# Moving the load and decoding of one piece of w_in behind unit 2's values, and giving unit 3's second value tile its own room, in a block-sparse attention and ELU feed-forward kernel on one core

## The chip, the cores and the metric

The kernel runs on one core of one Trainium2 chip. The time is the device time of one launch in microseconds (us): the median of several runs. A profile is one further execution, recorded by the hardware profiler.

## What is computed

Four sequences of 768 tokens with 8 heads of 64 attend under a block mask (blocks of 32: a window of one block to each side, the first and last block, and three sampled blocks per row of blocks). Its output, 3072 tokens of 512, goes through two dense layers with an ELU between.

```python
scores = scale * np.matmul(q, k.transpose(0, 1, 3, 2))
scores = np.where(mask, scores, -1000000000.0)
attn = np.exp(scores - np.max(scores, axis=-1, keepdims=True))
attn = attn / (np.sum(attn, axis=-1, keepdims=True) + 1e-09)
x = np.matmul(attn, v)          # then heads beside each other: 3072 x 512
h = x @ w_in                    # 512 x 2048
g = np.where(h > 0.0, h, np.exp(np.minimum(h, 0.0)) - 1.0)
return g @ w_out                # 2048 x 512
```

## The kernel before

The work is cut into 24 *units* of 128 query rows (two neighbouring blocks of 32 from two sequences). Unit 0 is a special one (the first and the last block); units 1, 2, 3 and so on are ordinary. Two units make one tile of 256 tokens for the dense layers. Matrix products in full precision are made of three 16-bit products, so every operand is split into a high and a low 16-bit part.

An ordinary unit `u` has these operations, called by short names: `q{u}` loads its queries; `vt{u}` and `vt{u}/2` load the two value tiles (one per block) on SP's queue, and `vg{u}`, `vg{u}/2` gather their sampled rows by an indirect DMA on GpSimd (POOL); `kg`, `kw` collect the keys on POOL; `s{u}.0`, `s{u}.1` are the score products on TensorE (PE); `mx` (row maximum, VectorE, DVE), `mb` and `ex` (bias and exponential, ScalarE, ACT), `pt` (transpose, PE), `ph`, `pl` (16-bit parts, DVE) follow; `av{u}.0`, `av{u}.1` are the products with the values; `nl`, `nx` scale them; `xt`, `xh`, `xl` turn and split the result. Then `h` and `o` are the two dense layers, with `a1` to `a5` for the ELU.

The weights come in 8 pieces of w_in (`wl0` to `wl7`) and 8 of w_out (`wl8` to `wl15`), 1 MB each. A piece is loaded by SP (`wl`), then decoded in place: `wu` (ACT) writes the common room `ZB`, `wb` (DVE) merges it, `wh` (ACT) makes the high part, `wlo` (DVE) the low part. The dense layers use the piece only after `wlo`.

The program is written for five engines (PE, ACT, DVE, POOL, SP). A planner (class `Plan`) puts all operations into one list, and each engine executes its own operations strictly in the order of that list; waits between engines are added from what is read and written. All loads of SP go through one hardware queue; SP has eight completion semaphores for them, and a load waits until the load eight before it has landed.

Value tiles live in three rooms of `VT`, taken in turn (`next_slot`, line 985); unit 1 alone uses two rooms in `GR` (slots 3 and 4, line 1227). A tile that takes a room of `VT` waits for the products of the unit that used that room. The first load of a room also brings the last block's rows (lines 1229 to 1232), so it is three DMAs of 130, 130 and 390 KB instead of one of 390 KB; the gather brings 96 rows of 4160 bytes more. `ST` is a staging room: it holds zeros at the very start and is taken next by the piece `wl14`.

PE's order around the change is: `s1.0`, `s1.1`, `pt1.0`, `pt1.1`, `s2.0`, `pt1.2`, `pt1.3`, `av1.0`, `s2.1`, `pt2.*`, `av2.*`, `s3.0`, `pt3.*`, `h0.0` (first dense product), `s3.1`, `av3.0`, `av3.1`, `s4.0` and so on; the dense layers of the first two tiles are then mixed into the attention of later units.

Of the kernel before, what the change touches and what calls it, by code (L numbers as in the profile page):

```python
# [11 lines left out]
F16 = mybir.dt.float16  # L12
# [339 lines left out]
}  # L352

LATENCY = 0.05
TAIL = {"DVE": 0.08, "ACT": 0.09}
LANDING = 1.8
DMA_FROM = 3.4
# [31 lines left out]
class Plan:  # L389
# [32 lines left out]
    def order(self):  # L422
# [14 lines left out]
        for op in reversed(self.ops):  # L437
# [4 lines left out]
            for d in {*op.deps, *op.after}:  # L442
                need = min(d.where.values()) + (d.dma + LANDING + d.slack if d.dma else 0.0) + LATENCY
                d.prio = min(d.prio, op.prio - need)
# [18 lines left out]
        def left_at(b):  # L463
# [3 lines left out]
            for o in (*b.writers, *b.readers):  # L467
                if o.end is None:
                    return None
                at = max(at, o.end + LATENCY)  # L470
            return at
# [30 lines left out]
        def enter(op):  # L502
# [5 lines left out]
            for e in op.where:  # L508
                op.at[e] = max([at] + [
                    d.end + (0 if d.eng == e and not d.dma else LATENCY) for d in op.deps])  # L510
                bisect.insort(waiting[e], (op.prio, op.n, op))
# [33 lines left out]
        while left:  # L545
            moved = False
            for eng, ops in waiting.items():
# [61 lines left out]
                if eng == "SP" and op.dma:  # L609
                    while ring and ring[0][0] <= t + dur:  # L610
                        ring.pop(0)
                    while ring and sum(n for _, n in ring) + op.pk > RING:
                        dur = max(dur, ring.pop(0)[0] - t)
                free[eng] = t + dur - (min(TAIL[eng], 0.3 * dur) if eng in TAIL else 0.0)
                op.end = t + dur
                if op.dma:
                    dma_free = max(dma_free, op.end) + op.dma
                    op.end = dma_free + LANDING + max(0.0, RANK["LATE"][TO(op)])
                    if eng == "SP":
                        ring.append((dma_free, op.pk))  # L620
                        landed += [dma_free + LANDING] * op.nd
                        heapq.heappush(events, dma_free - RANK["BACK"])
                for e in (free[eng], op.end + LATENCY, op.end):
                    heapq.heappush(events, e)
# [22 lines left out]
        return done  # L647

    def run(self):
        for _, op in self.order():  # L650
            for b in op.new:
                b.ap = b.make()
            op.fn(op.eng)
# [3 lines left out]
def kernel(  # L657
# [63 lines left out]
    def const(shape, dtype, name):  # L721
        return sb.tile(shape, dtype, tag=name, name=name)
# [40 lines left out]
    ST = const([P, 2, RW], I32, "ST")  # L763
    ZB = const([P, 2 * DM], I32, "ZB")
    nc.gpsimd.memset(ZB, 0)
    VV = [VT[:, 2 * i : 2 * i + 2] for i in range(3)]
    VV += [GR[:, y * 4 * RW : (y + 1) * 4 * RW].rearrange("p (c b x) -> p c b x", c=2, b=2) for y in range(2)]
    idx = const([P, NB], I32, "idx")
    cols = const([1, NPAIR, (NB - 2) * NR], I32, "cols")

# [214 lines left out]
    def next_slot():  # L985
        slot_n[0] += 1
        return (slot_n[0] - 1) % 3
# [90 lines left out]
    def unit(u):  # L1078
        g, i = u // NUP, firsts[u // NUP][u % NUP]
        two = (i, i + 1) if i else (0, NB - 1)  # L1080
        return g, i, [(x, n) for x in range(2) for n in two]
# [21 lines left out]
    spare = 1 if unit(0)[1] == 0 else 0  # L1103
# [58 lines left out]
    def attention(u, t, via, due):  # L1162
# [34 lines left out]
        elif sp:  # L1197
# [8 lines left out]
            for c in range(NKC):  # L1206
                vt = vts[c // 2]

                def load(e, c=c, vt=vt):
                    dst = VV[vt.slot][:, c % 2].rearrange("p b x -> p (b x)")  # L1210
                    r0 = BLK + c * P
                    if c < NKC - 1:
                        nc.sync.dma_start(dst, vd[g].ap[r0 : r0 + P, :])
                    else:
                        nc.sync.dma_start(dst[0:64], vd[g].ap[r0 : r0 + 64, :])
                        nc.sync.dma_start(dst[64:P], vd[g].ap[NB * BLK :, :])
                plan.add({"SP": 0.5}, tv, load, r=[vd[g]], w=[vt], dma=1.9, name=f"vt{u}",
                         nd=1 if c < NKC - 1 else 2)
            vin = vts
        else:  # L1220
            for y in range(2):
                i = i0 + y
                vt = Buf("VG" if u == spare else "VT", lambda: None)
                vin.append(vt)

                def load(e, i=i, vt=vt, y=y):
                    vt.slot = 3 + y if u == spare else next_slot()
                    two = VV[vt.slot].rearrange("p c b x -> p c (b x)")
                    if in_room.get(("v", vt.slot)) != g:
                        in_room["v", vt.slot] = g  # L1230
                        nc.sync.dma_start(two[96:P, 0, :], vd[g].ap[NB * BLK : (NB + 1) * BLK, :])
                        nc.sync.dma_start(two[0:BLK, 1, :], vd[g].ap[(NB + 1) * BLK :, :])
                    nc.sync.dma_start(two[BLK:P, 1, :], vd[g].ap[(i - 1) * BLK : (i + 2) * BLK, :])
                whole = first_in_room[u == spare] > 0
                first_in_room[u == spare] -= 1
                plan.add({"SP": 1.5 if whole else 0.6}, tv, load, r=[vd[g]], new=[vt], dma=2.7 if whole else 1.62, slack=RANK["SLACK"][2], name=f"vt{u}", nd=3 if whole else 1)

                def gather(e, i=i, vt=vt):
                    nc.gpsimd.indirect_dma_start(  # L1239
                        VV[vt.slot][0:96, 0].rearrange("p b x -> p (b x)"), None, vd[g].ap,  # L1240
                        bass.IndirectOffsetOnAxis(ap=idx[0:96, i : i + 1], axis=0))
                mark["vt", u] = plan.add({"POOL": 1.0}, tv, gather, r=[vd[g]], w=[vt], dma=1.65, slack=RANK["SLACK"][2], name=f"vg{u}")
# [456 lines left out]
```

## Time and profile before

| | us |
|---|---|
| median of 3 runs | 720.19 |
| lowest, highest run | 718.27, 724.62 |
| the profiled execution, its own time | 717.76 |
| its span, first to last instruction | 715.8 |
| PE busy | 675.0 |
| mean granted clock of PE | 0.984 of full |

The profiled execution's span is 2.0 us shorter than its own time, and that time is 2.4 us under the median of the three runs.

### The profile page before, as it was taken

Reading aid. Unit: us, or ns where it says so; the run is one execution under the profiler, and the core shown is the slowest. Engines: PE = TensorE matmul, PEld = TensorE weight load, DVE = VectorE, ACT = ScalarE, POOL = GpSimd, SP = SyncE. Lnnn points to the kernel's source line nnn. Section 1 sums busy time; section 2 is a strip of 40 time slices with the busy share of each in tenths; the row PEclk is TensorE's granted clock in tenths of the full one; section 3 lists DMA queues with packets and bytes.
Section 4 is the critical chain, followed back from the end, with each engine's and each line's share of the span. In section 5 each row is a group of like instructions: output and inputs, shape, how many; then the busy total and the mean of one; then the engine's idle time right before and its main releaser. Section 6 shows DMA issues by size and latency. Waiting matters only on the chain.

```text
span 715.8 us, 23435 instructions
## 1 busy us (share of the span) xinstructions
PE 675.0 (94%) x9586; PEld 452.0 (63%) x9586; DVE 457.1 (64%) x896; ACT 405.4 (57%) x815; POOL 212.4 (30%) x446
## 2 busy tenths in 40 slices
PE   8786779999999999999999999999999999999997
PEld 5564447666566567577567577587576476586673
DVE  4677798997667667667678567665367466354140
ACT  2765379895666556547377457365366365453250
POOL 2327255541022551100663432302044334000000
PEclk9997899999999999999999999999999999999999
DMA  8999999999899998877579998979669987871001
GB/s 194 241 365 224 252 288 246 245 208 252 201 207 208 195 173 158 172 188 186 114 107 187 185 187 154 165 152 196 120 120 209 183 133 126 149 114 31 16 2 30
DMA packets 200780, 123.18 MB, mean 172 GB/s; under 512 B 155936, under 2 KB 184736, under 8 KB 199904
## 3 DMA queue, kind: packets, MB, share of 16 engines
q1 hardware_dynamic: 195664, 103.98, 70.9%
q0 software_dynamic: 4928, 17.57, 10.4%
q8 instruction: 75, 1.23, 0.8%
q14 instruction: 33, 0.27, 0.1%
q10 hardware_dynamic: 80, 0.13, 0.0%
HBM read 76.98 MB, written 13.21 MB: 126 GB/s over the span
## 4 chain that ended last, share of the span: by engine, by line
PE 80%; DMA 6%; DVE 5%; issue 3%; ACT 3%; SPq 2%; POOL 0%; POOLq 0%; ACTq 0%; DVEq 0%
PE h L1559 32%; PE o L1585 28%; PE av L1459 6%; PE s L1585 3%; PE s L1346 3%; PE s L1355 3%; DMA wi<-in_moe_w_in_dram 2%; DMA VT<-vd,idx 1%; DMA vd<-ST 1%; SPq L945 1%; DMA wi<-in_k_dram 1%; PE av L1585 1%; PE s L1334 1%; DMA st<-in_k_dram 1%; DVE ST L1030 1%
## 5 line engine op out<-in xcount | busy, mean ns | idle before, releaser
L1559 PE MATMUL h<-xT,wi 128*128 128x256 f16 x2304 | 266.3, 273 | 5.9 <-DVE FE L1567 4.1
L1559 PEld LDWEIGHTS <-wi 128*128 128x128 f16 x2304 | 221.5, 98 | 47.2 <-issue 8.5
L1585 PE MATMUL o<-wo,GR 128*128 128x512 f16 x960 | 219.0, 379 | 0.1
L1585 PEld LDWEIGHTS <-GR 128*128 128x128 f16 x1152 | 109.6, 98 | 126.1 <-issue 5.0
L1286 POOL COPY kG<-kT 128x128 int32 x264 | 90.7, 380 | 154.3 <-PE s L1355 47.4
L1567 DVE SCALAR_TENSOR_TENSOR FE<-h,FE 128x512 f32<-128x512 f32 x96 | 65.4, 688 | 67.6 <-ACT FE L1572 67.3
L1388 DVE TENSOR_REDUCE m<-s 128x2 f32<-128x512 f32 (+1 forms) x104 | 65.4, 663 | 36.9 <-PE s L1355 20.4
L1156 DVE TENSOR_TENSOR p<-e,p 128x512 f16<-128x512 f32 x84 | 60.6, 721 | 42.8 <-ACT p L732 42.2
L1570 ACT ACTIVATE FE<-h 128x512 f32<-128x512 f32 x96 | 56.4, 594 | 55.6 <-PE h L1559 53.6
L1120 ACT ACTIVATE e<-s,m 128x256 f32<-128x256 f32 x176 | 73.4, 470 | 21.3 <-DVE p L1156 19.8
L1239 POOL DMA_INDIRECT VT<-vd,idx x42 | 43.2, 1029 | 140.1 <-PE av L1459 133.5
L1572 ACT ACTIVATE FE<-FE,gs 128x512 f32<-128x512 f32 x96 | 68.6, 721 | 2.0
L1577 DVE TENSOR_TENSOR GR<-FE,GR 128x512 f16<-128x512 f32 x86 | 62.2, 738 | 11.2 <-ACT GR L732 9.9
L732 ACT ACTIVATE GR<-FE 128x512 f16<-128x512 f32 x74 | 45.6, 628 | 23.4 <-DVE FE L1567 23.1
L732 ACT ACTIVATE p<-e 128x512 f16<-128x512 f32 x70 | 43.8, 626 | 14.8 <-DMA pT<-p 14.6
L1459 PEld LDWEIGHTS <-pT 128*32 128x32 f16 (+1 forms) x3384 | 40.6, 99 | 17.9 <-issue 16.1
L1265 POOL COPY kG<-kT 128x384 int32<-128x384 int32 x88 | 48.8, 582 | 0.1
L1416 ACT ACTIVATE m<-m 128x2 f32<-128x2 f32 x90 | 17.8, 200 | 51.8 <-DVE m L1388 42.0
L1459 PE MATMUL av<-VT,pT 128*32 128x66 f16 (+4 forms) x3240 | 45.1, 206 | 1.7 <-DMA VT<-vd,idx 1.7
L732 ACT ACTIVATE ro<-o 128x512 f32<-128x512 f32 x17 | 10.1, 597 | 51.3 <-PE o L1585 47.6
L1346 PE MATMUL s<-kG,qT 64*32 64x256 f32 x704 | 29.6, 409 | 9.7 <-ACT FE L1120 4.5
L1585 PE MATMUL s<-wo,GR 128*128 128x512 f16 x144 | 33.7, 379 | 0.1
(164 smaller groups left out, 596.6 us busy)
## 6 DMA issues: line engine op xcount, KB each, us to landing
VT<-vd SPq DMA_DIRECT2D x42, 390.0 KB
st<-in_q_dram SPq DMA_DIRECT2D x44, 128.0 KB
out_dram<-ro SPq DMA_DIRECT2D x43, 128.0 KB
wi<-in_moe_w_in_dram SPq DMA_DIRECT2D x4, 1023.0 KB
wi<-in_k_dram SPq DMA_DIRECT2D x8, 384.0 KB
wo<-in_v_dram SPq DMA_DIRECT2D x6, 512.0 KB
st<-in_v_dram SPq DMA_DIRECT2D x12, 256.0 KB
st<-in_k_dram SPq DMA_DIRECT2D x12, 256.0 KB
```

The lines of the kernel that those rows point to most:

```text
L732: nc.scalar.activation(dst, src, AF.Copy, scale=scale)
L1120: nc.scalar.activation(e32.ap[:, y, :], s.ap[:, y, :], AF.Exp, bias=m.ap[:, 6 + y : 7 + y], scale=SC, accum_out=m.ap[:, 2 + y : 3 + y] if ...
L1156: plan.add(LO, rank + 1, margin=mo, fn=lambda e: ENG[e].tensor_tensor(p.ap[:, 1, :], got(), p.ap[:, 0, :], op=ALU.subtract), r=[e32, p], w ...
L1286: nc.gpsimd.tensor_copy(dst[:, :, r * W : (r + 1) * W], src[:, :, bass.ds(at[r], W)])
L1388: nc.vector.tensor_reduce(m.ap[:, at + i.start : at + i.stop], ss[c].ap[:, i], axis=AX.X, op=ALU.max, negate=True)
L1459: nc.tensor.matmul(av[half].ap[rs, at : at + w], lhsT=pts[d].ap[:, pl * 4 + y * 2 + z, rs], rhs=room[:, z, x, h * VW + v0 : h * VW + v0 + ...
L1559: nc.tensor.matmul(h.ap[:, a, :], lhsT=w[:, wl, cs], rhs=x.ap[:, xl, cc, :], start=(n == 0), stop=(n == 3 * NCC - 1))
L1567: nc.vector.scalar_tensor_tensor(e32.ap, h.ap, -IH * GS, e32.ap, op0=ALU.mult, op1=ALU.min)
L1570: plan.add({"ACT": 0.6}, p0, lambda e: nc.scalar.activation(e32.ap, h.ap, AF.Exp, scale=IH), r=[h], new=[e32], name=f"a1{U}.{f2}")
L1572: plan.add({"ACT": 0.72}, p0, lambda e: nc.scalar.activation(e32.ap, e32.ap, AF.Relu, bias=gs_col, scale=-GS), r=[e32], w=[e32], name=f"a2 ...
L1577: plan.add(LO, p0, margin=mo, fn=lambda e: ENG[e].tensor_tensor(g.ap[:, 1], e32.ap, g.ap[:, 0], op=ALU.subtract), r=[e32, g], w=[g], name= ...
L1585: nc.tensor.matmul(o.ap, lhsT=g.ap[:, gl, f % 2, m * P : (m + 1) * P], rhs=wo[:, part, wl, (f % 2) * DM : (f % 2 + 1) * DM], start=(f == 0 ...
```

## The change

Nine operations are taken out of the planner's list and put back behind another one; in addition the second value tile of unit 3 gets the room `ST` (slot 5) in place of the next room of `VT`.

```diff
+MOVES = [
+    ("wl1", "vt2/2"), ("vt3/2", "vt3"), ("vg3/2", "vg3"), ("wu1", "xh1"), ("wb1", "xl1"),
+    ("wh1", "wb1"), ("wlo1", "mx3.0/2"), ("vt4/2", "vt4"), ("vg4/2", "vg4")]
+EXTRA = 3
...
     def run(self):
-        for _, op in self.order():
+        line = [op for _, op in self.order()]
+        named = {op.key: op for op in line}
+        for key, behind in MOVES:
+            line.remove(named[key])
+            line.insert(line.index(named[behind]) + 1, named[key])
+        for op in line:
...
+    VV.append(ST.bitcast(F16).rearrange("p c (b x) -> p c b x", b=2))
...
-                    vt.slot = 3 + y if u == spare else next_slot()
+                    vt.slot = 3 + y if u == spare else 5 if u == EXTRA and y else next_slot()
```

What this does to each engine's order (PE's doesn't change):

```
SP    before: wl1 q4 vt1 vt1/2 vt2 vt2/2 vt3 q5 q6 wl9 wl2 vt3/2 vt4 wl10 q7 wl3 wl12 vt4/2 vt5
SP    after:  q4 vt1 vt1/2 vt2 vt2/2 wl1 vt3 vt3/2 q5 q6 wl9 wl2 vt4 vt4/2 wl10 q7 wl3 wl12 vt5
POOL  before: vg3 kg3.0 kw3.0 kg3.1 kw3.1 kg4.0 vg3/2 vg4 kw4.0 kg4.1 kw4.1 kg5.0 kw5.0 vg4/2 vg5
POOL  after:  vg3 vg3/2 kg3.0 kw3.0 kg3.1 kw3.1 kg4.0 vg4 vg4/2 kw4.0 kg4.1 kw4.1 kg5.0 kw5.0 vg5
ACT   before: wh8 wu1 mb1.0 mb1.0/2 ex1.0 ex1.1 wh1 mb1.1 ... nl2.0 xh1 nl2.1 mb3.0 ex3.0
ACT   after:  wh8 mb1.0 mb1.0/2 ex1.0 ex1.1 mb1.1 ... nl2.0 xh1 wu1 wh1 nl2.1 mb3.0 ex3.0
DVE   before: mx1.0/2 wlo8 wb1 mx1.1 mx1.1/2 ph1.0 wlo1 ph1.1 ... nx2.0 xl1 mx3.0 mx3.0/2 nx2.1
DVE   after:  mx1.0/2 wlo8 mx1.1 mx1.1/2 ph1.0 ph1.1 ... nx2.0 xl1 wb1 mx3.0 mx3.0/2 wlo1 nx2.1
```

Unit 3's second tile is the first value tile in `ST`, so its load also brings the last block's rows, three DMAs in place of one. One room of `VT` fewer is taken by unit 3, so unit 4's second tile waits for unit 2's products in place of unit 3's; from unit 5 on each tile waits for the same products as before. `wl14` now waits for unit 3's products.

## Rows read from the trace of the kernel before

**Rows 1.** The page, part 1: busy time of each engine in the span.

```profile
PE 675.0 (94%) x9586; PEld 452.0 (63%) x9586; DVE 457.1 (64%) x896; ACT 405.4 (57%) x815; POOL 212.4 (30%) x446
```

**Rows 2.** Busy time by stretch; then PE's granted clock, DMA share, GB/s.

```profile
57.00:62.00 5.00, 0.63 (x9) 0.14 (x8) 2.96 (x4) 2.24 (x6) 3.22 (x10) 0.90 1.04 207
62.00:70.00 8.00, 7.12 (x73) 3.85 (x74) 6.66 (x11) 4.75 (x14) 5.51 (x11) 0.64 1.04 241
...
75.00:78.00 3.00, 0.00 (x0) 0.00 (x0) 0.87 (x2) 0.00 (x0) 0.00 (x0) 1.00 1.03 242
...
87.00:106.00 19.00, 14.22 (x318) 9.33 (x310) 18.02 (x32) 13.27 (x30) 8.99 (x23) 0.91 0.92 280
...
110.00:211.00 101.00, 100.95 (x1252) 68.03 (x1251) 80.01 (x136) 75.55 (x130) 33.66 (x61) 1.00 0.96 229
```

**Rows 3.** What PE waited for, 40 to 120 us: total, times, longest.

```profile
PE s L1346 <- ACT FE L1120: 4.5, 1, 4.5
...
PE s L1346 <- issue: 3.2, 1, 3.2
PE av L1459 <- DMA VT<-vd,idx: 1.7, 1, 1.7
```

**Rows 4.** The chain of work that ended last, 57 to 62.5 us.

```profile
46.37 13.31 DMA wi<-in_moe_w_in_dram
...
60.98 0.23 ACT m L1416 x2
...
62.08 0.63 PE s L1346
```

**Rows 5.** Timeline, unit 1: start, duration, engine, work, idle before it.

```profile
57.65 0.69 DVE L1388 TENSOR_REDUCE m<-s 128x2 f32<-128x512 f32 x1 [0.44 <-PE o L1182]
...
65.70 1.22 DVE L897 TENSOR_TENSOR wi<-wi 128x1024 f16<-128x1024 f32 x1
...
67.44 1.28 DVE L1150 TENSOR_TENSOR pT<-h,pT 128x512 f16<-128x512 f32 x2
...
70.61 0.95 PE L1459 MATMUL av<-GR,pT 128*32 128x130 f16 x71 [0.96 <-issue]
```

**Rows 6.** What SP's queue waited for, 30 to 140 us.

```profile
SPq L1233 <- PE av L1459: 8.7, 2, 5.5
...
SPq L1233 <- DMA wi<-in_moe_w_in_dram: 4.6, 1, 4.6
```

**Rows 7.** Timeline of SP: loads as they were issued.

```profile
59.69 0.30 SPq L1233 DMA_DIRECT2D GR<-vd  x1
...
79.79 1.77 SPq L879 DMA_DIRECT2D wo<-in_moe_w_out_dram  x1
81.60 0.47 SPq L875 DMA_DIRECT2D wo<-in_moe_w_in_dram  x1
87.66 1.94 SPq L1233 DMA_DIRECT2D VT<-vd  x2
```

**Rows 8.** DMA view: queue of instruction fetches, 75.3 to 75.4 us (packets, MB, share).

```profile
q8 instruction: 1, 0.02, 80.6%
```

**Rows 9.** DMA view, 81.2 to 92.2 us: rate in 40 equal slices.

```profile
GB/s 83 62 28 141 62 92 160 372 417 432 387 432 432 447 365 380 409 409 402 409 409 402 402 379 298 112 15 257 136 151 378 333 136 197 106 106 227 333 392 315
```

**Rows 10.** Timeline of ACT and DVE, units 2 and 3.

```profile
85.63 0.60 ACT L732 ACTIVATE xT<-h 128x512 f16<-128x512 f32 x1 [0.24 <-PE h L1527]
...
86.50 0.68 DVE L1540 TENSOR_TENSOR xT<-h,xT 128x512 f16<-128x512 f32 x1
87.12 1.29 DVE L1388 TENSOR_REDUCE m<-s 128x2 f32<-128x512 f32 x2
...
89.85 1.36 ACT L732 ACTIVATE ZB<-wo 128x1024 f16<-128x1024 bf16 x1
...
94.44 1.22 DVE L890 SCALAR_TENSOR_TENSOR wo<-wo,ZB 128x1024 int32<-128x1024 int32 x1
...
100.63 0.36 DVE L734 COPY low<-av 128x192 f32<-128x192 f32 x1 [0.57 <-PE av L1459]
```

## The prediction

> **What bounds the kernel now.** I read the busy times first: PE is busy for 675 of 716 us [rows 1], so the time is PE's work plus the holes in it. Then the stretches, to see where the holes lie. From 110 to 211 us PE is busy for 100.95 of 101 us, although DMA, DVE and ACT are loaded too [rows 2]. So a microsecond that PE gains before 110 us should reach the end, and a microsecond lost there as well. Before 110 us PE is nearly empty in two places: 57 to 62 us (0.63 us busy) and 75 to 78 us (0.00 us) [rows 2]. The list of PE's waits gives their sizes: 4.5 us on an exponential of ACT, 3.2 us with no releaser shown, and 1.7 us on a gather into a value tile [rows 3].
>
> The first hole has a chain [rows 4]: the load of w_in's piece 1 (wl1) takes 13.31 us and lands at 59.68; only then does ACT run wu1, which stands in its queue ahead of unit 1's bias, so that the bias comes at 60.98 and s1.1 goes on at 62.08. The maxima that the bias needs were complete at 57.65 + 0.69 = 58.34 [rows 5]. SP stands behind the same load: the last load of unit 1's second value tile waited 4.6 us for it and was issued at 59.69 [rows 6, 7], and the products with that tile begin at 70.61 after 0.96 us of waiting [rows 5]. From 87 to 106 us another engine is the bound: DVE is busy for 18.02 of 19 us [rows 2].
>
> **Unit 1, what is removed.** Two paths lead to av1.0, and the later one counts. By calculation: the bias can start at 58.4, 2.6 us earlier, and DVE loses wlo1 (1.22 us) ahead of the low parts that end at 67.44 + 1.28 = 68.72 [rows 5]; together 3.8 us. The other decoding step of DVE, wb1, lay beside the wait and gives nothing more. PE could have run av1.0 at 70.61 - 0.96 = 69.65, so this path comes to 65.8. Its bounds are 2.6 us (the exponential alone) and about 5 us, because 62 to 70 us ran at a granted clock of 0.64, partly the 1.2 GHz level after the hole [rows 2], and a shorter hole may spare some of that. By data: SP no longer waits 4.6 us, so the tile comes to 66.0. I take the later, **-4.6 us**.
>
> The second hole follows, inside s2.1 and not at its begin. In it the DMA view shows one packet of the queue of instruction fetches, moving at 75.3 us [rows 8]; I read the hole as PE waiting for its own instructions. If that fetch is asked for by PE's progress, it moves along with PE and the hole keeps its 3.2 us; bounds: the hole stays where it is (rival 1) or closes (rival 3). I take the move, since the DMA engines are as loaded before it as they will be (1.04 of their time at 62 to 70 us [rows 2]).
>
> The Trainium skill, "DMA: Bandwidth & Descriptors", section "Queues, rings and completion order", says that a DMA engine takes turns between the queues that have work for it, packet by packet. By that rule a fetch isn't held behind the whole backlog of SP's loads, which speaks against rival 1; the hole in the trace shows only that the fetch was late, not what it stood behind.
>
> **Units 2 and 3, what is added.** The decoding now stands behind xh1 and xl1. xh1 ends at 85.63 + 0.60 = 86.23, wu1 takes 1.36 us, to 87.59; xl1 ends at 86.50 + 0.68 = 87.18 [rows 10], so DVE waits 0.4 us for wu1. wb1 takes 1.22 us [rows 10] and wlo1 1.22 us [rows 5]. Queued behind them on DVE are mx3.0 and nx2.1, and from there DVE has hardly a gap until 106 us. On ACT, wh1 waits for wb1, and nl2.1, mb3.0 and ex3.0 stand behind it; this runs beside DVE's delay and is shorter than it. The cost is 0.4 + 1.22 + 1.22, **+2.85 us**. It would be 0 to 1.2 us if DVE had room there; in the row of mx3.0 it follows xl1 with no idle time [rows 10], so I keep the upper end. wl1 itself now has until 86.23 - 4.6 = 81.6 us; its bytes stand behind unit 2's tiles, which are complete in SP's queue before q5, so I charge nothing, with 0 to 2 us as bounds.
>
> **Unit 3's second tile.** Its load waited for unit 2's products (8.7 us in two waits of this line [rows 6]) and was issued at 87.66 [rows 7]; now it goes with vt3. PE's wait of 1.7 us goes [rows 3], but DVE paces that place: what it gains is the 0.57 us that it sat idle before nl3.0 [rows 10]. **-0.6 us**. On POOL one gather moves ahead of kg3.0; POOL is busy for less than half of 87 to 106 us [rows 2], so it costs nothing, and under 1 us if the keys were late. vt4/2 moves ahead of wl10 and its gather ahead of kw4.0: nothing waited for either. wl14 waits for unit 3's products, which end long before it is issued.
>
> **What stands behind the moved loads.** vt3/2 is now ahead of q5, q6, wl9 and wl2, and it is a whole load: 160 rows of 4160 bytes from SP and 96 from the gather, 1.07 MB, at the 241 GB/s of 62 to 70 us [rows 2] 4.4 us. wl9 and wl2 show as the stretch near 400 GB/s from 83.1 to 88 us [rows 9], so wl9 ends about 85.6. The lull before (seven slices at a quarter of that rate, [rows 9]) gives back up to 1.5 us, and the 1 MB that wl1 leaves open near 50 us, where the queue may run dry, costs up to 3: wl9 lands at 88.5 to 91.5. It is wanted: DVE comes to wb9 at 94.44 - 4.6 + 2.85 = 92.7, and wu9 ahead of it takes 1.36 us [rows 10], so it must be there by 91.3. I charge **+0.2 us** (0 to 2).
>
> **Sum.** -4.6 + 2.85 - 0.6 + 0.2 = -2.1 us at 106 to 110 us. Behind that PE has no holes until 211 us, so nothing is lost by the rows; 0 to 2 us could be, if a weight then comes too late for an earlier PE, and I take 0. The profiled execution, 717.76 us, becomes 715.6; the median, 2.4 us above it, becomes 720.19 - 2.1 = 718.1 us.
>
> **Rivals.**
> 1. *The second hole doesn't move; slower.* If PE still resumes at 78 us, because the fetch stands behind the backlog of loads, the first gain is gone and the decoding in units 2 and 3 is paid: +2.85 - 0.6 = +2.3, 722.5 us. It decides from a resumption later than 78.0 - 2.3 = 75.7. For it: the late fetch itself, and DMA engines full on both sides [rows 2, 8].
> 2. *wl9 becomes the late one.* Every us beyond 91.3 is lost on ACT and DVE; from 93.4 nothing is left, at 94.3 it is 721 us. For it: wl1 took 13.31 us in the same queue [rows 4]. Against it: wl9 is small against the lull that is filled. The Trainium skill, same page, section "Why a DMA increments its semaphore by 16 and not by 1", says that a load counts as landed only when each of its engines has finished, so one slow engine delays all of it; by that rule wl9 would land later than the mean rate says. No row here shows the engines singly.
> 3. *The second hole closes as well.* The loads in flight are smaller without wl1, so the fetch comes in time: -2.1 - 3.2, 714.8 us. Against it: the same bytes are moved by 80 us.
> 4. *The gain is lost behind 110 us*: 720.2 us. Against it: PE's full stretch [rows 2].
>
> **How the numbers follow.** Forecast 0.42 (its own range 716 to 720), rival 1 0.16, rival 2 0.12, rival 3 0.20, rival 4 0.10. The predicted time is the forecast's, 718.1. The range takes in rival 3's 714.8 less 1 us and rival 1's 722.5 plus half a microsecond; the runs of before alone spread over 6 us: 713.8 to 723. A change under 1% (7.2 us) is about what a measurement of this kernel can't tell from none. Faster by that much needs rival 3 and a larger first gain (half of rival 3's chance): 0.10. Slower by it needs rivals 1 and 2 together: 0.04. Same: 0.86.
>
> **What would show it.** In the changed kernel's profile: no wait of 4.5 us at s1.1 but one near 2 us (57.6 to 59.6); av1.0 near 66; PE's hole of 3.2 us inside s2.1 ending near 73.5; wu1 near 81.6 with no wait on its load; DVE full from 82 us on; no wait of av3.0 on its gather; wu9 without a wait on wl9, at 88 to 90 us; PE full from about 108 us. I am wrong if the hole still ends at 78, if ACT waits for wl9 or wl1 for more than 1 us, or if the time from 110 us to the end grows by what was gained before.

## The result

| | before | changed |
|---|---|---|
| median | 717.55 us (21 runs) | 719.09 us (21 runs) |
| ratio, 95% interval | | 1.0051 [1.0028, 1.0075] |
| profiled execution, its own time (span) | 717.76 (715.8) | 715.86 (713.9) |

The kernel became about half a per cent slower where 0.3 % faster was forecast. The profiled execution of the changed kernel was the fastest of its 21 runs, so its span says nothing on the change; I read it by places, not by its end. Two more profiles of the changed kernel and three more of the kernel before (below) show what is usual. Some executions of any kernel run over 1.5 % above its fastest; all ratios leave these out (the medians over all 21 runs differ by 0.2 %), and in k1 and c2 below the profiled execution was such a one, so only their ratios are used. A second series of the unaltered changed kernel (e1 below) gave 1.0012 [0.9967, 1.0057]: that there is no gain of 0.3 % rests on the first series, and the size of the loss is uncertain.

The page of the changed kernel, part 1 (compare [rows 1]):

```profile
PE 672.1 (94%) x9586; PEld 451.6 (63%) x9586; DVE 455.8 (64%) x896; ACT 405.7 (57%) x815; POOL 211.4 (30%) x446
```

Busy time by stretch, changed kernel (compare [rows 2]; the last three columns are PE's granted clock, DMA share, GB/s):

```profile
57.00:62.00 5.00, 3.57 (x52) 1.71 (x49) 4.35 (x7) 3.26 (x11) 3.68 (x10) 1.00 1.02 226
62.00:70.00 8.00, 5.94 (x157) 4.06 (x159) 6.58 (x12) 3.71 (x11) 6.63 (x18) 1.00 1.04 251
70.00:75.00 5.00, 0.99 (x20) 0.38 (x24) 1.64 (x3) 0.04 (x1) 0.83 (x2) 0.77 1.04 276
75.00:78.00 3.00, 2.07 (x49) 0.79 (x41) 1.99 (x8) 1.32 (x5) 0.82 (x3) 0.50 1.05 277
87.00:106.00 19.00, 14.94 (x318) 9.81 (x310) 18.30 (x32) 13.12 (x27) 9.58 (x24) 0.84 1.04 296
110.00:211.00 101.00, 100.86 (x1251) 67.78 (x1249) 80.08 (x136) 76.02 (x133) 32.31 (x58) 1.00 0.96 228
```

What PE waited for, 40 to 120 us (compare [rows 3]):

```profile
PE s L1356 <- issue: 4.0, 1, 4.0
PE s L1142 <- ACT e L1130: 3.3, 3, 1.7
PE av L1469 <- issue: 2.7, 2, 1.8
PE av L1469 <- DMA GR<-vd,idx: 1.9, 1, 1.9
...
PE s L1356 <- ACT FE L1130: 1.6, 2, 1.2
```

The first part went as forecast: the hole at 57 us is nearly gone (PE 3.57 of 5 us busy against 0.63), s1.1's wait is 1.2 us in place of 4.5, av3.0's wait on its gather is gone. But the wait with no releaser inside s2.1 is 4.0 us (before 3.2), and a second one of 1.8 us stands inside av2.0. The stretch with nearly no work has only moved, from 75 to 78 us to 70 to 75 us. The timeline of PE gives the places: s1.1 and av1.0 ahead, then av2.0 behind its hole, s3.0 and the first dense product h0.0 (compare [rows 5]):

```profile
59.11 1.07 PE L1356 MATMUL s<-kG,qT 64*32 64x256 f32 x24 [1.19 <-ACT FE L1130]
...
66.35 0.84 PE L1469 MATMUL av<-GR,pT 128*32 128x130 f16 x54 [1.86 <-DMA GR<-vd,idx]
...
83.37 0.24 PE L1469 MATMUL av<-VT,pT 128*32 128x66 f16 x3 [1.76 <-issue]
...
85.36 1.96 PE L1356 MATMUL s<-kG,qT 64*32 64x256 f32 x32
...
92.60 1.75 PE L1569 MATMUL h<-xT,wi 128*128 128x256 f16 x12
```

In the DMA view a packet of the queue of instruction fetches goes ahead of the end of each hole. It starts at 71.9 and at 80.3 us and ends 1.5 us before PE goes on; the two windows are 71.9 to 72.0 us and 80.3 to 80.4 us (compare [rows 8]):

```profile
q8 instruction: 1, 0.02, 75.9%
...
q8 instruction: 1, 0.02, 96.7%
```

The chain of waits shows the load of piece 1, now 21.67 us under way (13.31 before, [rows 4]), then a load of q5 that SP could issue only behind it; SP's timeline gives wl9 at 84.46 (79.79 before, [rows 7]):

```profile
59.92 21.67 DMA wi<-in_moe_w_in_dram
...
81.60 4.98 DMA st<-in_q_dram
```

```profile
72.50 11.15 SPq L1109 DMA_DIRECT2D st<-in_q_dram  x4
84.46 2.51 SPq L889 DMA_DIRECT2D wo<-in_moe_w_out_dram  x1
```

**Where the lead goes.** I sorted PE's matmuls and weight loads by start and counted. Whatever the kernel, the holes that follow such a fetch packet lie at the same counts, if there is one: 1704 (inside s2.1), 1957 (inside av2.0), 2211, 2463, 2718, which are 252 to 255 apart. The list of waits gives most of them no releaser, and those at 2718 one that differs from run to run, even for the same kernel. (PE also stands with no releaser at 1408, 1427 and 2546 in some profiles, 0.6 to 1.3 us, with no such packet ahead; these aren't counted.) I read the five counts as the borders between blocks of instructions that PE fetches one at a time. 1451 is the border before them. The means of four profiles of the kernel before and three of the changed one, in us at which PE passes each place:

```
                 s1.1   1451   1704   1957   2211   2463   2718  o0.1.0  48 matmuls on
before (4)       62.0   71.4   77.4   83.5   90.1  100.8  107.1  110.0   115.9
changed (3)      59.4   66.9   74.9   83.9   93.6  101.4  107.7  112.3   118.7
difference       -2.6   -4.5   -2.5   +0.4   +3.5   +0.6   +0.6   +2.3    +2.8
```

The lead of 4.5 us is gone by 1957. And the fetches that belong to the first two borders: PE's entry into the block ahead, the begin of the next fetch packet after it (in brackets how long after the entry), the passing of the border, and the hole at it (from the start of one instruction to that of the next, so 0.2 to 0.4 us more than in the list of waits). The runs from e1 on are explained in the next section:

```
                enters  fetch       passes 1704 hole   fetch       passes 1957 hole
before            70.7  75.4 (+4.6)   78.0  3.5        79.7 (+1.7)   84.7  0.0
b1_before         71.7  74.6 (+2.9)   77.2  0.0        80.2 (+2.9)   83.0  0.8
b2_before         72.0  73.5 (+1.5)   76.9  0.0        79.3 (+2.3)   82.9  0.0
b3_before         71.2  74.8 (+3.6)   77.5  2.6        80.5 (+2.9)   83.5  0.3
changed           66.5  71.9 (+5.4)   74.7  4.4        80.3 (+5.7)   83.4  2.0
e1_same           67.1  72.3 (+5.2)   75.1  4.1        81.2 (+6.0)   84.1  2.7
a2_after          67.1  72.4 (+5.2)   74.9  2.6        81.4 (+6.4)   84.2  2.6
e2_decode_only    66.1  71.2 (+5.1)   73.8  3.7        79.5 (+5.7)   82.5  2.0
e3_room_only      68.8  74.3 (+5.5)   77.0  3.5        82.4 (+5.4)   85.1  2.2
e4_wl9_first      66.5  71.6 (+5.1)   74.2  3.5        80.2 (+5.9)   82.7  2.7
n1_no_decode      68.1  73.1 (+5.0)   75.7  2.4        81.2 (+5.5)   84.0  2.2
n2_no_piece       67.2  72.9 (+5.7)   75.6  3.4        81.0 (+5.4)   84.0  1.8
c1_after_piece9.. 65.2  70.4 (+5.1)   72.9  3.9        78.6 (+5.7)   81.6  2.0
k2_same_no_piece  67.9  73.0 (+5.2)   75.7  2.9        78.5 (+2.8)   82.4  0.0
k3_after_room...  66.8  71.4 (+4.6)   73.9  3.3        78.9 (+5.0)   81.9  2.2
k4_unit3_values.. 67.4  72.7 (+5.2)   75.3  4.1        78.6 (+3.3)   83.6  0.0
k5_before_value.. 68.6  74.3 (+5.7)   77.2  4.5        81.9 (+4.8)   85.5  0.0
k6_after_queries. 66.3  71.1 (+4.8)   73.7  2.4        78.6 (+4.8)   81.2  1.4
```

Summed over the first four borders the holes are 3.6, 1.2, 0.1 and 3.1 us in the kernel before (mean 2.0) and 7.6, 7.0 and 5.6 us in the changed one (mean 6.7): 4.7 us more, as much as unit 1 gained. In these two blocks a fetch that starts 5 to 6 us after PE's entry costs a hole; one that starts 1.5 to 3.3 us after it costs at most 0.8 us. In between it depends on how long PE needs for the block (k5 took 8.3 us for its second one and shows no hole). Every hole of over 1 us at these two borders ends 1.2 to 1.7 us behind the end of its packet, in all profiles; this is what ties the holes to the fetches.

### The profile page after: what moved, and what is told of

It is laid out like the page before. It is cut to its first block, busy times and chain, and to the rows that moved or that the text cites. A ratio compares the mean times of both kernels' runs of the same rounds, so it can differ in the third digit from the quotient of the medians.

```text
span 713.9 us, 23435 instructions
## 1 busy us (share of the span) xinstructions
PE 672.1 (94%) x9586; PEld 451.6 (63%) x9586; DVE 455.8 (64%) x896; ACT 405.7 (57%) x815; POOL 211.4 (30%) x446
## 3 DMA queue, kind: packets, MB, share of 16 engines
q8 instruction: 75, 1.23, 0.7%
## 4 chain that ended last, share of the span: by engine, by line
PE 62%; DMA 14%; DVE 9%; issue 4%; ACT 4%; SPq 3%; POOLq 2%; POOL 1%; DVEq 0%; ACTq 0%
PE h L1569 25%; PE o L1595 22%; DMA pT<-p 4%; PE av L1469 4%; PE s L1595 3%; DMA wi<-in_moe_w_in_dram 3%; PE s L1356 2%; POOLq L1292 2%; DMA xT<-n 1%; DVE m L1398 1%; SPq L955 1%; DMA VT<-vd,idx 1%; DVE FE L1577 1%; PE s L1365 1%; DMA wi<-in_k_dram 1%
## 5 line engine op out<-in xcount | busy, mean ns | idle before, releaser
L1249 POOL DMA_INDIRECT VT<-vd,idx x41 | 40.7, 992 | 143.1 <-PE av L1469 136.9
```

## The experiments

In all diffs the list MOVES is that of the change unless shown; each ratio is to the kernel before, run on the same chip.

**Which part is it.** Theory A at this point: late fetches, the decoding on DVE and a late wl9 together eat the first gain. The expectations call the start of o0.1.0, a group of products just before PE fills up, the mark.

```diff
 e1_same: the changed kernel, unaltered
 e2_decode_only
-EXTRA = 3, moves of vt3/2 vg3/2 vt4/2 vg4/2
+EXTRA = -1, only the moves of wl1 wu1 wb1 wh1 wlo1
 e3_room_only
-moves of wl1 wu1 wb1 wh1 wlo1
+only the moves of vt3/2 vg3/2 vt4/2 vg4/2, EXTRA = 3
 e4_wl9_first
+    ("wl9", "vt3")
```

> The changed kernel again, unaltered, for a second profile and more times. The mark is the start of o0.1.0 (the group of 6 matmuls of 512 columns just before PE fills up, at 109.28 us before and at 110.38 us in the first profile of the changed kernel). Theory A (the first gain is real but is eaten by two holes in which PE waits for its instructions while the DMA engines are full, and the decoding and a late wl9 then cost more than is left): both holes again, 4 us inside s2.1 and 2 us inside av2.0, ACT waiting 1 to 2 us for wl9, mark 109.9 to 111. Rival B (the mark is where it was and the time grows behind 110 us): mark at 108 to 109.3. Ratio to before 1.002 to 1.008 by both.

> Only the five moves of piece 1 (load and decoding); unit 3's second tile and unit 4's stay where they were, in rooms of VT. Theory A: unit 1 gains its 4 us, the DMA engines run empty near 80 us as before, so there is no hole inside av2.0 (or one under 0.5 us) and no wait for wl9; av3.0 waits for its gather; the decoding still costs 2 to 3 us: mark 108.3 to 109.8, ratio 0.995 to 1.002. Rival C (the decoding in DVE's full stretch is the whole loss, the loads don't matter): mark 110 or later, ratio 1.003 to 1.008.

> Only the room of unit 3's second tile and the four moves of the value tiles; piece 1 is loaded and decoded where it was before. Theory A: the hole at s1.1 (4.5 us) is there, the DMA engines don't run empty near 80 us, a hole of 1 to 2 us inside av2.0 appears, wl9 comes at 91 to 93 and ACT waits for it up to 3 us; av3.0 doesn't wait: mark 109 to 111, ratio 1.000 to 1.006. Rival C: no loss without the decoding, mark 107.6 to 108.7 (1.7 us of av3.0's wait or DVE's 0.6 us gained), ratio 0.997 to 1.000.

> All nine moves, and wl9 taken ahead of unit 3's second tile in SP's queue. Theory A: ACT's wait for wl9 (1.46 us) goes; the DMA engines are as full, so the holes inside s2.1 and av2.0 stay: mark 109 to 110 (0.5 to 1.4 us earlier than the changed kernel), ratio 1.000 to 1.005. Rival 2 of the prediction alone (wl9's lateness is the whole loss): mark 108 to 109, ratio 0.996 to 1.000.

Measured: e1 1.0012 [0.9967, 1.0057], e2 1.0044 [1.0012, 1.0076], e3 1.0014 [0.9972, 1.0055], e4 1.0056 [1.0017, 1.0094]; marks 113.1, 111.0, 110.6 and 113.9, of which theory A had only e3's. In e4 wl9 goes out at 67.4 us and ACT no longer waits for it; this brings nothing, so its lateness is not the cause (rival 2 of the prediction falls). e2 came out as rival C said, and n1 below tests that rival. Each part alone loses its lead at the same two borders: e2 leads by 3.6 us at 1704 (73.8 against 77.4) and by 1.0 at 1957; e3, whose lead is 0.4 us at 1704, is 1.6 us behind at 1957, with piece 1 in its old place. So an early PE isn't needed for the late fetch: the earlier load of unit 3's tile alone does it too.

e3 missed at s1.1 as well: 4.5 us of waiting were expected there, since piece 1 hadn't moved, but its load came in at 57.3 us (59.3 to 59.8 in the kernel before) and PE waited 1.6 us:

```profile
57.41 1.37 ACT L743 ACTIVATE ZB<-wi 128x1024 f16<-128x1024 bf16 x1 [0.35 <-DMA wi<-in_moe_w_in_dram]
...
59.75 1.07 PE L1358 MATMUL s<-kG,qT 64*32 64x256 f32 x24 [1.62 <-ACT FE L1132]
```

e3 and k5 below, both without the move of piece 1, enter the block at 1451 2.6 and 2.8 us ahead of the kernel before. What brings the load in earlier there is open, and so is how much of unit 1's gain the move of piece 1 is worth.

**Was the first profile of before usual (one execution each).** Theory D: its hole at s1.1 was unlucky and is usually under 3 us.

```diff
 b1_before, b2_before, b3_before: the kernel before, unaltered
 a2_after: the changed kernel, unaltered
```

> The kernel before, unaltered, for its profile alone. Its first profile had a hole of 4.5 us at s1.1 (the load of piece 1 landed at 59.7 us) and the mark o0.1.0 at 109.3 us. Theory D (that hole was an unlucky execution, its usual size is 1.5 to 2.5 us, so the change had less to gain than I took): the hole under 3 us, piece 1 used by ACT at 57 to 58.5 us, av1.0 at 68 to 69.5 us. Rival (the hole is as large in every execution and the change loses elsewhere): 4 to 5 us again, av1.0 at 70 to 71 us.

> As b1_before: a further execution of the kernel before. Theory D: the hole at s1.1 under 3 us and the mark within 1.5 us of the other profiles of this kernel. Rival: 4 to 5 us.

> As b1_before: a further execution of the kernel before. Theory D: the hole at s1.1 under 3 us. Rival: 4 to 5 us.

> The changed kernel, unaltered, a third profile. Theory D with theory A: s1.1 with 1.6 us of waiting as in both profiles so far, a hole of about 4 us inside s2.1 and of about 2.5 us inside av2.0, the mark o0.1.0 at 110 to 113.5 us, later than in the profiles of the kernel before by 1 to 3 us.

What PE waited for in b1, 40 to 120 us:

```profile
PE av L1459 <- DMA VT<-vd,idx: 4.1, 1, 4.1
PE s L1346 <- ACT FE L1120: 3.1, 1, 3.1
...
PE av L1459 <- DMA GR<-vd: 2.0, 1, 2.0
...
PE av L1459 <- issue: 0.6, 1, 0.6
```

The wait at s1.1 is 3.1 to 3.5 us there and s1.1 resumes at 61.7 to 62.2 us: usual, so theory D falls. The hole inside s2.1 is not: 3.5, 0, 0 and 2.6 us. And av3.0 waits 3.0 to 4.1 us for its gather, not 1.7. The sum was made against one execution, and at two of its terms that one was off by 1 to 2 us. a2 has its mark at 113.4 us, within what was expected, and two holes of 2.6 us, the first smaller than the 4 us expected.

**What the decoding costs, and what the load costs.**

```diff
 n1_no_decode (n1 and n2 leave out work; the dense layer reads piece 0 where it read piece 1)
-wu1, wb1, wh1, wlo1
 n2_no_piece
-wl1, wu1, wb1, wh1, wlo1
```

> The changed kernel without the decoding of w_in's piece 1 (wu1, wb1, wh1, wlo1 are left out, the load stays; the dense layer uses piece 0 in place of piece 1). Theory A, that from 85 to 107 us DVE sets the pace in the changed kernel and the decoding in it eats the first gain: DVE loses 2.45 us of work and the 0.6 us that it stood before wb1, wb9 comes 2 to 3 us earlier (93.6 to 95 in place of 96.6), and o0.1.0 stands at 109 to 110.5 in place of 110.4 to 113.4 (mean 112.3); ratio to the kernel before 0.997 to 1.000. Rival, that the loads behind unit 2's values are what comes too late (wl9 lands at 92.5): wu9 and wb9 stay where they are, o0.1.0 at 111.5 or later, ratio 1.003 or more.

> The changed kernel with neither load nor decoding of piece 1 (the dense layer uses piece 0 in its place): 1 MB less in SP's queue between 60 and 82 us. Theory A, with late instruction fetches caused by the backlog of loads: PE's hole inside s2.1 falls from 2.3 to 4.0 us to 1.5 us or less and the one inside av2.0 (1.8 to 2.5 us) goes; wl9 is issued 3 us or more earlier; o0.1.0 at 105 to 107.5, the end 5 us or more below the changed kernel's (ratio 0.992 to 0.995). Rival, that the fetch is late whatever SP loads: the two holes keep 2 us or more each and only the decoding's 3 us are gained, o0.1.0 at 109 to 110.

Measured: n1 1.0051 [1.0011, 1.0092], o0.1.0 at 110.8; n2 1.0006 [0.9967, 1.0044], o0.1.0 at 109.6. With the decoding taken out the kernel is no faster within the noise of half a per cent, where theory A wanted 0.997 to 1.000; the mark comes at the early end of the changed kernel's 110.4 to 113.4, and wb9 stays where it was (96.7 against 96.6 us). So theory A as I had it falls. DVE's timeline in n1 shows why, in the idle time in brackets:

```profile
84.64 0.16 DVE L1505 TENSOR_SCALAR r<-av 128x4 f32<-128x4 f32 x1 [2.08 <-ACT low L743]
...
87.98 1.29 DVE L1400 TENSOR_REDUCE m<-s 128x2 f32<-128x512 f32 x2 [1.34 <-PE s L1358]
...
90.93 0.69 DVE L745 CAST pT<-s 128x512 f16<-128x512 f32 x1 [0.66 <-PE s L1144]
...
95.50 1.29 DVE L1400 TENSOR_REDUCE m<-s 128x2 f32<-128x512 f32 x2 [0.76 <-PE s L1358]
```

DVE now stands 4.8 us in 82 to 96 us in these four waits for a PE that is late from its holes; the 2.45 us of decoding fit into that. n2 tells the load: without the 1 MB the ratio falls by 0.45 %, about 3 us, which is at the edge of the noise of the two. But the two first holes stay (3.4 and 1.8 us; 1.5 or less and none were expected), and the mark is at 109.6, not at 105 to 107.5: this is what the rival had, that the fetch is late whatever SP loads. I put it down to the value tile of unit 3, 1.07 MB, which has taken the place; k2 below, where that tile comes later, bears this out for the second hole alone.

In the changed kernel's profile PE comes out of those holes at the lower clock. Busy time by stretch, first the changed kernel, then n1, then b1 (column PEclk as above):

```profile
80.00:84.00 4.00, 2.24 (x75) 1.89 (x75) 1.89 (x3) 0.33 (x1) 0.00 (x0) 0.50 1.05 210
84.00:88.00 4.00, 4.00 (x108) 2.24 (x106) 3.13 (x7) 2.01 (x3) 0.46 (x2) 0.50 1.24 167
88.00:92.00 4.00, 2.27 (x18) 1.80 (x11) 3.90 (x9) 3.04 (x8) 2.74 (x6) 0.50 0.96 348
```

```profile
84.00:88.00 4.00, 4.00 (x79) 2.24 (x82) 1.73 (x6) 0.93 (x2) 0.00 (x0) 0.50 1.19 182
88.00:92.00 4.00, 2.94 (x51) 2.70 (x47) 3.24 (x8) 2.19 (x7) 2.46 (x7) 0.50 1.02 331
```

```profile
80.00:84.00 4.00, 3.23 (x112) 2.18 (x114) 3.90 (x12) 1.55 (x6) 1.67 (x5) 1.00 0.93 122
84.00:88.00 4.00, 2.87 (x105) 1.97 (x91) 3.71 (x10) 2.46 (x8) 1.36 (x6) 1.00 0.95 370
88.00:92.00 4.00, 3.83 (x56) 2.61 (x55) 3.97 (x7) 1.39 (x2) 3.44 (x8) 1.00 1.08 308
```

From 80 to 92 us the changed kernel is granted 1.2 GHz (0.50), b1 2.4 GHz. b1 is the best of its four: the others were granted 0.50 to 0.73 from 80 to 84 us and 0.74 to 0.89 from 84 to 88, and 1.00 from 88 to 92. The changed kernel's second profile (e1) is at 0.50 throughout as well, its third (a2) between 0.50 and 1.00. The 32 products of s3.0 take 1.96 us in the one and, in b1's timeline, 1.09 us:

```profile
84.17 1.09 PE L1346 MATMUL s<-kG,qT 64*32 64x256 f32 x32
```

So s3.1 starts at 94.3 us (90.2 in b1), and from its maximum on DVE has hardly a gap up to o0.1.0 in the changed kernel; in b1 it stands once for 3.0 us, behind av3.0's wait for its gather.

**Taking DVE's work out of 87 to 107 us instead.**

```diff
 c1_after_piece9_late: MOVES of the change, and
 c2_before_piece9_late: these alone, EXTRA = -1
+    ("wu9", "ph4.1"), ("wb9", "pl4.1"), ("wu10", "ex4.3"), ("wb10", "wu10"),
+    ("wh9", "ex4.3"), ("wlo9", "wh9"), ("wu3", "a21.0"), ("wb3", "a31.0"),
+    ("wh3", "a10.1"), ("wlo3", "a51.0")
```

> The changed kernel with the decoding of w_out's piece 9 moved behind 107 us (pieces 10 and 3 one turn later), so that DVE has 2.44 us less to do between 87 and 107 us. Theory A: o0.1.0 comes 2 to 2.5 us earlier than in the changed kernel (about 110 in place of 112.3), and some of it is given back from 110 to 126 us, where DVE had only 1.6 us idle at one place: end 0 to 2.4 us below the changed kernel's. Rival, that DVE isn't what sets 85 to 107 us there: o0.1.0 at 111.5 or later.

> The kernel before with the same move of piece 9's decoding. Theory A: in the kernel before the same stretch waits for unit 3's second value tile (av3.0 1.7 to 4.1 us on its gather, to 99 to 102 us), not for DVE alone, so o0.1.0 moves by 0 to 1 us (109.3 to 110.5 before), and the end is the same or up to 2 us later. Rival, that DVE sets this stretch in both kernels alike: o0.1.0 2 us or more earlier, at 107 to 108.5.

Measured: c1 1.0143 [1.0085, 1.0200], o0.1.0 at 113.1; c2 1.0106 [1.0052, 1.0161]. It came out as the rival said and worse: 2.44 us less of DVE does not bring the mark forward, since the fetch for 2718 came 6.1 us after PE's entry, with a hole of 5.0 us; behind 110 us more was lost, which I put down to the moved decoding without having shown it. DVE alone does not set this stretch. c2 lost more than the 2 us expected at most.

**Is it the fetch.** Theory F: a fetch is served early where SP's loads have just run dry and about 5 us late where other loads fill that lull.

```diff
 k1_room_behind_wl9: the kernel before, EXTRA = 3 and
+    ("vt3/2", "wl9"), ("vg3/2", "vt3/2")
 k2_same_no_piece: k1 without wl1, wu1, wb1, wh1, wlo1 (leaves out work; piece 0 in place of piece 1)
 k3_after_room_behind_wl9: k1 and the moves of wl1, wu1, wb1, wh1, wlo1
 k4_unit3_values_behind_wl9: the moves of wl1, wu1, wb1, wh1, wlo1 and
+    ("vt3", "wl9"), ("vt3/2", "vt3"), ("vg3", "vt3/2"), ("vg3/2", "vg3")
 k5_before_values_behind_wl9: the four moves of k4 alone, EXTRA = 3
```

> The kernel before with unit 3's second tile in its own room, its load put behind wl9 and its gather behind that, nothing else moved (piece 1 in its old place). Theory F (a block of 256 PE instructions is fetched while the one ahead of it runs, and the fetch is served 0.6 to 2.4 us after PE comes into that block when SP's loads have just run dry, as at 79 to 81 us in the kernel before, and 4.4 to 5.4 us after it when other loads fill that lull, as in the changed kernel): the fetch near 80 us stays at +3 us or less, PE has no hole over 1 us inside av2.0, mx3.1 starts at 91 to 93.5 as before, and without av3.0's wait for its gather (1.7 to 4.1 us before) o0.1.0 stands 1.5 to 3 us earlier than before's mean of 110.0; ratio 0.995 to 0.999. Rival, that any earlier load of this tile costs what it gains: fetch at +4 us or more or wl2 and wl9 late, o0.1.0 at 110 or later, ratio 1.000 to 1.004.

> The kernel k1_room_behind_wl9 without piece 1's load and decoding (the dense layer uses piece 0 in its place), so 1 MB less in the queue from 46 to 80 us, and PE early at s1.1 as in the changed kernel. Theory F: the loads run dry some 4 us earlier, so the fetches of the blocks that PE meets inside s2.1 and inside av2.0 come at +3.5 us or less and the two holes are together 3 us or less (4.1 to 6.3 us in the changed kernel's runs); o0.1.0 at 107 or earlier, ratio 0.990 to 0.995. Rival, that the fetch takes about 5 us behind PE whatever is loaded: both fetches at +4.4 us or more, holes of 4 us or more together, o0.1.0 at 108.5 or later.

> The changed kernel with unit 3's second tile loaded behind wl9 and not ahead of q5 (unit 4's tile in its old place): the decoding behind unit 2's values as in the change. Theory F: PE comes to the blocks 3 to 4 us earlier than in the kernel before, but the loads run dry no earlier, so the fetch near 80 us is again served at 79 to 81 us, +4 us or more after PE's entry, and the hole inside av2.0 stays at 1.5 us or more; wl9 is issued near 79 us, o0.1.0 at 110 to 112, ratio 1.000 to 1.004. Rival, that the early load of unit 3's tile alone spoils the change: no hole over 1 us inside av2.0, o0.1.0 at 107 to 108, ratio 0.994 to 0.998.

> The changed kernel with both value tiles of unit 3 (their loads and gathers, 2.1 MB) put behind wl9, so that the loads run dry before PE comes to the block of instructions inside av2.0; piece 1 and its decoding as in the change, unit 4's tile in its old place. Theory F: the fetch that PE met inside av2.0 comes at +3 us or less after PE's entry (4.4 to 5.4 us in the changed kernel), no hole over 1 us inside av2.0, the granted clock from 84 to 92 us is 0.9 or more in place of 0.50, wl9 is issued by 77 us; o0.1.0 at 106.5 to 109 (112.3 in the mean of the changed kernel's profiles, 110.0 before), ratio 0.993 to 0.998. Rival, that the fetch takes about 5 us whatever is queued: a hole of 1.5 us or more inside av2.0, the clock at 0.5 to 0.7 behind it, o0.1.0 at 110 or later, ratio 1.000 or more. Rival, that unit 3's values now come too late: av3.0 waits 2 us or more on DMA, o0.1.0 at 110 or later.

> The kernel before with the same move of unit 3's value tiles and with the room of its own, piece 1 in its old place. Theory F: PE comes to its blocks as late as before (s1.1 at 62, s2.1 at 77 to 78), the fetch near 80 us at +2 us or less, the clock at 0.85 or more from 84 to 92 us, and the gather wait of av3.0 (1.7 to 4.1 us before) under 1.5 us; o0.1.0 at 108 to 110 (110.0 before), ratio 0.996 to 1.000, that is 2 us or more behind k4_unit3_values_behind_wl9, which has unit 1's wait removed as well. Rival, that moving piece 1 brings nothing even with a free queue: this kernel as fast as that one within 1 us.

Measured: k1 0.9994 [0.9959, 1.0029], between theory F and its rival; k2 0.9973 [0.9940, 1.0006], o0.1.0 at 108.5; k3 1.0026 [0.9984, 1.0068], 110.6; k4 1.0033 [0.9998, 1.0068], 113.4; k5 1.0031 [0.9997, 1.0066], 111.1.

For the border at 1957 theory F held: in k3 wl9 went out at 77.75 us and the fetch still started only at 78.9, 5.0 us after the entry, with 2.2 us of hole; in k2, with 1 MB less queued, and in k4, with unit 3's tiles out of the way, it started 2.8 and 3.3 us after it and the hole was gone. The fetch for 1704 stayed 5.2 us late in both. What did not follow either is the time. PE's waits and the stretches of k2 and of k4:

```profile
PE s L1359 <- issue: 2.5, 1, 2.5
...
PE h L1572 <- issue: 1.9, 1, 1.9
```

```profile
80.00:84.00 4.00, 4.00 (x130) 3.09 (x136) 3.27 (x8) 1.37 (x4) 1.83 (x3) 0.69 1.03 278
84.00:88.00 4.00, 2.89 (x85) 1.99 (x66) 3.81 (x10) 2.62 (x8) 1.69 (x7) 1.00 1.05 251
```

```profile
PE s L1364 <- issue: 4.6, 3, 3.8
PE s L1150 <- ACT e L1138: 4.0, 3, 2.4
PE s L1364 <- DVE x L1516: 3.5, 1, 3.5
```

```profile
80.00:84.00 4.00, 2.98 (x77) 2.05 (x76) 2.48 (x4) 0.05 (x2) 2.33 (x4) 0.50 1.02 273
84.00:88.00 4.00, 3.76 (x108) 2.31 (x108) 2.80 (x6) 2.16 (x3) 0.46 (x1) 0.65 1.05 211
```

With the hole at 1957 gone, k2 has its clock back by 84 us but stands 1.9 us at the next border, 2211 (in h0.0, fetch 5.5 us after the entry). k4 is at the lower clock from the hole at 1704 up to about 86 us, waits for exponentials that stand behind the decoding on ACT, and meets a fetch 5.0 us late and a hole of 3.9 us at 2718; the list of waits puts that hole down to DVE's x (in other runs to ACT's p, m or low), but in the changed kernel's profile and in k2, k3, k4 and k6 alike it ends 1.5 to 1.7 us behind the end of the fetch packet. k5 misses its own expectation in the same way (4.5 us at 1704), and with piece 1 in its old place it is as fast as k4 (1.0031 against 1.0033): its rival, that moving piece 1 brings nothing, came out. PE reached s1.1 at 60.3 us there, not at the 62 expected, as in e3. Of the orders of the loads tried here none that holds the whole work is measurably faster than the kernel before.

**What the fetch is late behind.** Over 85 fetches of 17 profiles the start came 3.0 us after the entry (median, 16 fetches) where the packets moved in the first 1.5 us were under 700 bytes in the mean, and 5.2 us (57 fetches, 48 of them at 4.4 or more) where they were over 2000; 12 lie between.

```diff
 k6_after_queries_first: MOVES of the change, and
+    ("q5", "vt2"), ("q6", "q5")
```

> The changed kernel with the query loads q5 and q6 (small packets, 250 to 410 bytes in the mean where they ran) put behind unit 2's first value tile, ahead of its second and of wl1. Over 85 fetches of 17 profiles the fetch started 3.0 us (median) after PE's entry into the block ahead where the packets moved then were under 700 bytes in the mean, and 5.2 us where they were over 2000. Theory P, that the size of the packets counts: if the small packets run at 66 to 70 us, when PE comes to the block that ends inside s2.1, that fetch comes at +4 us or less (5.2 to 5.4 in the changed kernel's profiles) and the hole inside s2.1 is 2 us or less; the next one, behind value tiles alone, stays at +4.4 us or more with its hole of 2 us or more. o0.1.0 at 110 to 113, ratio 1.000 to 1.006. Rival, that only the amount queued counts: both fetches at +4.4 us or more and both holes of 2 us or more.

Measured: 1.0071 [1.0040, 1.0103], o0.1.0 at 112.9. The small packets ran from 64 to 68 us; PE entered the block at 66.3 and the fetch started 4.8 us later, among large packets again, hole 2.4 us. That misses theory P (4 us, 2 us) by little and does not meet its condition for the whole wait; the rival has both fetches right (4.8 us each) but not the second hole (1.4 us): inconclusive. The first two holes were the smallest of the kernels that hold the whole work of the change and its early start, the fetch for 2718 was 5.7 us late with a hole of 4.7 us, and the kernel is the slower for it.

## Why the prediction was wrong

Its terms, against the means of the profiles at the borders:

| step | forecast | measured |
|---|---|---|
| unit 1 (to 1451) | -4.6 | -4.5 |
| hole inside s2.1 moves along (1451 to 1704) | 0 | +2.0 |
| next fetch, inside av2.0 (1704 to 1957) | not in the sum | +2.9 |
| decoding in units 2 and 3 (1957 to 2211) | +2.85 | +3.1, most of it not the decoding |
| unit 3's second tile (2211 to 2463) | -0.6 | -2.9 |
| wl9, and the rest to o0.1.0 | +0.2 | +1.7 |
| sum at o0.1.0 | -2.1 | +2.3 |

**The step that failed** is the one on the second hole: "If that fetch is asked for by PE's progress, it moves along with PE and the hole keeps its 3.2 us". The mechanism was half right: in the means PE's entry came 4.5 us earlier and this fetch 2.4 us, so it moved along only in part, and the hole is 3.7 us where the kernel before has 1.5. And I treated it as one event. It recurs every 250 instructions or so, and the next fetch didn't move along at all: PE entered its block 2.5 us earlier and the fetch started 1.1 us later, 5.7 to 6.4 us after the entry in place of 1.7 to 2.9. At that time value tiles were being moved: in the 1.5 us after the entry the mean packet had 2.7 to 3.1 KB, in the kernel before, with query packets among them, 0.4 to 1.6 KB. Rival 1 had the mechanism one border too early: there PE resumed at 74.7, at the next one with nothing left. The reason I gave against it, that the DMA engines are as loaded before as after, is a mean over a stretch, and the fetch did not go by it.

**A second term** failed with it: for the moved load of piece 1 I charged nothing. n2 against n1 and k2 against k3 put it at about 3 us, each pair at the edge of its noise.

The rule of the Trainium skill that spoke against rival 1 ("DMA: Bandwidth & Descriptors", section "Queues, rings and completion order": an engine takes turns between its queues packet by packet) is not contradicted: a fetch did get through in 5 to 6 us, while wl1 took 21.67. But it gave no size, and I read "not behind the whole backlog" as "not later than before".

**The size of the second hole** was taken from one execution. It was 3.2 us on the list of waits; counted from start to start it is 3.5, 0, 0 and 2.6 us in four profiles. Also, of the 8.7 us that I gave as the wait of the load of unit 3's second tile, 5.5 us are that load's and the rest another's; no term rests on it.

**Decoding.** The price of 2.45 us of DVE was right (1.23 and 1.22 us in the profile) and its place was wrong: in n1 it bought nothing back. The term came out near its forecast by chance; by the trace what fills it is PE at 1.2 GHz behind two holes and the waits for exponentials that follow.

**Unit 3's second tile** was worth more than forecast at its place (the gather wait is 3.0 to 4.1 us in three of four executions, not 1.7), but 1.7 us of it are lost again by o0.1.0. Whether DVE, the engine I named as the pace there, takes them is not shown: c1, with 2.44 us less of DVE's work, came no earlier.

**wl9** was late as the rival feared: wu9 waited 1.5 us for it. It cost nothing, because mx3.1, ahead of wb9 on DVE, was later still; in e4, without this wait, nothing was gained.

**Behind 110 us** PE stayed full (100.86 of 101 us), as forecast; what is lost by o0.1.0 agrees with the loss at the end: +2.3 to +2.8 us there, and 0.5 %, 3.7 us, with an interval from 2.0 to 5.4, in the first series of runs.

Shown by the runs: neither the decoding nor wl9 is the cause by itself (n1, e4, within half a per cent); less in the queue brings the fetch at 1957 in time (k2, k4). Indicated, at the edge of the noise: piece 1's load costs about 3 us (n2 against n1, k2 against k3). Argued from the traces only: that the blocks' borders are where I put them, that the holes at them are what eats unit 1's gain (without the one at 1957, k2 and k4 lost time at others), and that the lower clock makes the difference from 1957 to 2211. Open: what a fetch stands behind, how much of unit 1's gain comes from moving piece 1 (e3, k5), and whether any order of the loads carries that gain to the end.

## What to carry to other kernels

A gain ahead of a stretch in which the DMA engines are full may be lost to PE's instruction fetches, as it seems to be here: look for waits with no releaser, count the instructions between them, and check whether a faster PE comes to the next borders while large loads are still running. Removing a wait by moving a load moves 1 MB into another stretch as well; price that MB at the fetches and weights that share the queue's time, not at zero because a mean share stays the same. And before a hole of 3 us goes into a sum as a constant, look at it in a second and a third execution.

## What the hardware showed that I had not expected

PE's instruction fetches start up to 6.4 us after PE's entry into the block ahead (0.6 us at the least). The DMA view between entry and fetch, first the kernel before (78.1 to 79.7 us, fetch 1.7 us after the entry), then the changed one (74.8 to 80.2 us, 5.7 us), in packets, MB and share:

```profile
q1 hardware_dynamic: 820, 0.27, 104.3%
q0 software_dynamic: 17, 0.05, 11.1%
```

```profile
q1 hardware_dynamic: 389, 0.95, 77.6%
q0 software_dynamic: 121, 0.41, 27.8%
```

Both have the engines full (over 100 %); the first moves packets of some 330 bytes, the second of 2.4 KB and, on POOL's queue, 3.4 KB. So the share of busy DMA engines did not tell how long a fetch would take; the kind of packets goes with it, though k6 could not show that it is the cause.
